# Scores of two chunks made side by side in blocks of 32 keys, from unit two on

## The chip, the cores and the metric

The kernel runs on one core of one Trainium2 chip. The metric is the device time of one execution in microseconds (us); lower is better. TensorE is called PE in the profile (PEld is its weight load), VectorE is DVE, ScalarE is ACT, and SP is the engine whose queue issues the DMAs.

## The reference

Two blocks follow each other. The first is a gated linear recurrence over 768 steps for 4 batches and 8 heads of 48 channels, with a complex decay per channel; the second is a feed-forward block with an unusual activation.

```python
mag = np.sqrt(a_re * a_re + a_im * a_im)
scale = np.minimum(mag, 0.999) / (mag + 1e-06)
a_re_n, a_im_n = (a_re * scale, a_im * scale)
for t in range(S):                       # S = 768, D = 48, B = 4, H = 8
    ar, ai = (a_re_n[:, :, t, :, None], a_im_n[:, :, t, :, None])
    new_re = ar * S_re - ai * S_im
    new_im = ar * S_im + ai * S_re
    kv = np.einsum('bhd,bhe->bhde', k[:, :, t], v[:, :, t])
    S_re, S_im = (new_re + kv, new_im)
    y[:, :, t] = np.einsum('bhd,bhde->bhe', q[:, :, t], S_re)
...
x = np.ascontiguousarray(attn_out.transpose(0, 2, 1, 3)).reshape(B * S, H * D)
h = x @ w_in                             # 3072 x 384 times 384 x 2048
sp = np.maximum(h, 0.0) + np.log1p(np.exp(-np.abs(h)))
g = h * erf(sp)
return (g @ w_out).astype(np.float32)    # 3072 x 2048 times 2048 x 384
```

## The kernel before

The 3072 tokens are worked off in 12 units of 256 tokens; a unit is two chunks of 128 tokens (c = 0 and 1), and three units make one batch. In a chunk the recurrence is a masked product, as in linear attention: queries and keys are multiplied by running products of the decay (`prep`), which makes 96 rows per head (the real and the imaginary part of 48 channels). Their transposes come to stand in the tile `KQ` (96 rows, 16 heads' worth of keys and queries, 128 tokens). From unit 2 on this goes by a 32x32 block transpose on DVE and then 12 DMAs per chunk (`move`, four calls of three DMAs each, one call for each block of 32 tokens).

`scores(u, c, g)` takes one chunk and one group of four heads: four matmuls of 96 rows by 128 keys against 128 queries into one PSUM tile `sc` of the pool `ps_a` (two buffers), and then one DVE product of the whole tile with the upper triangle `triu` (keys not later than the query), written over the keys in `KQ`. A unit has four such steps, named A{u}.{c}.{g}. `state` (S) makes keys times values for a chunk and carries the sum on; `result` (Y) multiplies values with the masked scores, adds state times queries, and writes x transposed. In `state` and `result` the matmuls already have 32 columns in the array, and blocks that belong to different columns follow each other directly.

The feed-forward block of a unit is `ff_in` (h steps, 2 x 3 matmuls with 256 moving columns), activation work on ACT (x, G) and DVE (e), and the output products (O steps; from unit 3 on each is four matmuls of 192 columns, a scheme with seven instead of eight half products). Inputs are 32-bit floats. The profile shows each of these matmuls as two records, so a scores step is 8 records, an O step of units 3 and later 8, an h step 12.

No loop orders the work: the string `ORDER` names some 2,000 step parts, and each name runs the next part of that step's generator. So the order on every engine's queue, SP's included, is the order of that string: the first part of an A step issues the matmuls, the second the DVE product. `v` names load the values of a chunk, `M` names are the calls of `move`, `put` writes 128 tokens of the output with one DMA, and `u` names are matmuls that nobody reads.

Of the kernel before, what the change touches and what calls it, by code (L numbers as in the profile page):

```python
# [54 lines left out]
Q0.1 p0.1 A0.0.1 l1.1 l1.1 kT0.1.0 kT0.1.0 a1.0 l1.1 l1.0 l1.0 a1.1 a1.1 l1.0 A0.0.0 Q0.1 qT0.1.0 qT0.1.0 l1.1 p1.1
p1.1 p1.1 A0.0.0 kT0.1.1 kT0.1.1 a1.1 g2.0 g2.0 qT0.1.1 qT0.1.1 l1.0 p1.0 g2.1 t2 t2 Y0.0 Y0.0 n0 n0 n1 n1 n1 A0.1.0
A0.1.1 g2.1 t2 h0.0.4.0 n1 m2 t2 n5 n5 A0.1.0 n5 s1.0 q1.0 p1.0 Q1.0 n5 p1.0 v0.1 S0.1 k1.0 h0.0.0.0 l2 s1.0 s1.0 Q1.0
qT1.0.0 K1.0 s1.1 r2 A0.1.1 K1.0 n4 n4 p1.0 s1.1 Y0.1 l2 qT1.0.0 p0.1 h0.0.4.0 s1.1 h0.0.0.0 q1.1 Y0.1 Q1.1 qT1.0.1
qT1.0.1 n7 l2 n4 Q1.1 kT1.0.1 kT1.0.1 n4 n7 h0.0.4.1 S0.1 l2 l2 i3 k1.1 i3 kT1.0.0 kT1.0.0 h0.0.0.1 S0.1 h0.0.4.1 K1.1
A1.0.0 n7 v1.0 S1.0 l2 l2 A1.0.1 n6 A1.0.0 n7 n6 p1.1 h0.0.0.1 x0.0 K1.1 n6 A1.0.1 x0.0 x0.0 x0.0 h0.1.0.1 h0.1.0.1  # L60
h0.1.0.0 S1.0 n6 k2.0 p2.0 p2.0 a2.0 a2.0 a2.0 v1.1 S1.1 p1.0 S1.0 p2.0 qT1.1.0 qT1.1.0 kT1.1.1 kT1.1.1 e0.0.0 a2.0
a2.0 a2.0 n11 S1.1 kT1.1.0 e0.0.0 kT1.1.0 a2.0 e0.0.1 n10 v2.1 n10 h0.1.0.0 e0.0.1 G0.0 a2.1 a2.1 a2.1 Y1.0 Y1.0 n10
a2.1 p2.1 p1.1 v3.0 e0.0.0 qT1.1.1 qT1.1.1 h0.1.4.1 h0.1.4.1 A1.1.0 A1.1.0 a2.1 a2.1 a2.1 s2 s2 e0.0.1 A1.1.1 h0.1.4.0
v2.0 A1.1.1 h0.1.4.0 Y1.1 e0.0.1 n10 O0.1 g3.1 e0.0.0 s2 S1.1 Y1.1 g3.0 m3 g3.1 t3 K2.0 h1.0.6 K2.0 K2.0 p2.1 q2.0
# [1405 lines left out]
```

## Time and profile before

| | before |
|---|---|
| median of 3 runs | 641.28 us (640.8 to 641.76) |
| the profiled execution, its own time | 641.29 us |
| its span, first to last instruction | 639.5 us |
| PE busy | 629.0 us (98%), 5464 records |
| DVE busy | 585.5 us (92%) |
| ACT busy | 542.1 us (85%) |

The span is what the trace covers; the 1.8 us between it and the execution's own time lie around it. Busy time of PE includes the modelled ends of pipelined matmuls, so records overlap: what a group of matmuls costs is read from the start of one group to the start of the next, not from a record's duration.

### The profile page before, as it was taken

Reading aid. Unit: us, or ns where it says so; the run is one execution under the profiler, and the core shown is the slowest. Engines: PE = TensorE matmul, PEld = TensorE weight load, DVE = VectorE, ACT = ScalarE, POOL = GpSimd, SP = SyncE. Lnnn points to the kernel's source line nnn. Section 1 sums busy time; section 2 is a strip of 40 time slices with the busy share of each in tenths; the row PEclk is TensorE's granted clock in tenths of the full one; section 3 lists DMA queues with packets and bytes.
Section 4 is the critical chain, followed back from the end, with each engine's and each line's share of the span. In section 5 each row is a group of like instructions: output and inputs, shape, how many; then the busy total and the mean of one; then the engine's idle time right before and its main releaser. Section 6 shows DMA issues by size and latency. Waiting matters only on the chain. (4 is left out here: it accounts for less than half of the span.)

```text
span 639.5 us, 13517 instructions
## 1 busy us (share of the span) xinstructions
PE 629.0 (98%) x5464; PEld 555.0 (87%) x5464; DVE 585.5 (92%) x798; ACT 542.1 (85%) x674; POOL 1.1 (0%) x8
## 2 busy tenths in 40 slices
PE   7799999999999999999999999999999999999998
PEld 7589887877677888999998998898999998999998
DVE  6999999998999999999999799999989999986784
ACT  8999898999999989998894798899799978777840
POOL 0000000000000000000000000000000000000000
PEclk9899999999999999999999999999999999999999
DMA  8887676745357635543526744665564154410023
GB/s 215 196 235 185 143 143 153 209 62 108 57 123 132 179 51 124 107 84 71 99 39 173 149 76 74 155 120 82 127 115 75 26 112 71 73 22 26 1 89 113
DMA packets 282796, 70.27 MB, mean 110 GB/s; under 512 B 269396, under 2 KB 272488, under 8 KB 282728
## 3 DMA queue, kind: packets, MB, share of 16 engines
q1 hardware_dynamic: 282728, 69.36, 50.6%
q8 instruction: 44, 0.72, 0.5%
q14 instruction: 24, 0.20, 0.1%
HBM read 48.82 MB, written 4.75 MB: 84 GB/s over the span
## 5 line engine op out<-in xcount | busy, mean ns | idle before, releaser
L1181 PE MATMUL hps<-xT,w_in_sb 128*128 128x256 f32 (+1 forms) x1248 | 260.8, 364 | 0.3 <-ACT h L1184 0.2
L1181 PEld LDWEIGHTS hps<-xT,w_in_sb 128*128 128x128 f32 x1248 | 220.5, 190 | 29.1 <-ACT h L1184 1.8
L763 ACT ACTIVATE z<-z 128x2048 f32<-128x2048 f32 (+1 forms) x52 | 92.4, 1781 | 9.0 <-DVE e L1212 8.1
L762 ACT ACT_TABLE_LOAD x72 | 92.4, 1283 | 2.1 <-PEq L1454 0.9
L1212 DVE TENSOR_TENSOR e<-z,yy 128x1024 f32<-128x1024 f32 x48 | 58.5, 1218 | 13.1 <-ACT yy L763 12.5
L1184 ACT COPY h<-hps 128x512 f32<-128x512 f32 x96 | 54.3, 580 | 18.5 <-PE hps L1181 18.3
L1252 PE MATMUL ops<-w_out_sb,h 128*128 128x384 f32 x192 | 66.4, 490 | 0.0
L1216 DVE TENSOR_TENSOR z<-z,yy 128x1024 f32<-128x1024 f32 x48 | 58.0, 1219 | 4.4 <-ACT z L763 4.0
L763 ACT ACTIVATE z<-h 128x2048 f32<-128x2048 f32 (+1 forms) x26 | 46.3, 1781 | 15.9 <-DVE h L1218 12.6
L1214 DVE SCALAR_TENSOR_TENSOR yy<-e,yy 128x1024 f32<-128x1024 f32 x48 | 58.7, 1222 | 1.1
L1218 DVE SCALAR_TENSOR_TENSOR h<-z,h 128x1024 f32<-128x1024 f32 x48 | 58.2, 1220 | 1.0
L1252 PEld LDWEIGHTS ops<-w_out_sb,h 128*128 128x128 f32 x192 | 35.5, 190 | 20.9 <-DVE w_out_sb L825 0.6
L1106 PEld LDWEIGHTS sc<-KQ 96*128 96x128 f32 x384 | 48.1, 192 | 5.0 <-ACT KQ L1097 2.4
L1106 PE MATMUL sc<-KQ 96*128 96x128 f32 x384 | 49.8, 276 | 2.2 <-ACT KQ L1097 2.2
L763 ACT ACTIVATE yy<-z 128x2048 f32<-128x2048 f32 (+1 forms) x26 | 46.2, 1778 | 0.6
L763 ACT ACTIVATE yy<-yy 128x2048 f32<-128x2048 f32 (+1 forms) x26 | 46.2, 1777 | 0.5
L1166 PE MATMUL y<-KQ,v 128*32 128x128 f32 x768 | 32.7, 274 | 0.3 <-DVE Skv L1133 0.3
L1110 DVE TENSOR_TENSOR KQ<-sc,triu 128x512 f32<-128x512 f32 x48 | 32.5, 679 | 0.2 <-PE sc L1106 0.2
L1276 PE MATMUL X<-w_out_sb,h 128*128 128x192 f32 x144 | 26.4, 330 | 0.0
L1276 PE MATMUL Y<-T,S 128*128 128x192 f32 x144 | 26.1, 327 | 0.0
L1276 PE MATMUL Z<-T,h 128*128 128x192 f32 x144 | 25.9, 327 | 0.0
L1276 PE MATMUL Y<-w_out_sb,h 128*128 128x192 f32 x144 | 25.7, 326 | 0.0
(125 smaller groups left out, 1011.0 us busy)
## 6 DMA issues: line engine op xcount, KB each, us to landing
KQ<-X SPq DMA_DIRECT2D x240, 64.0 KB, 2.2
raw<-in_moe_w_in_dram SPq DMA_DIRECT2D x8, 768.0 KB
again<-in_moe_w_in_dram SPq DMA_DIRECT2D x8, 768.0 KB, 6.2
raw<-in_moe_w_out_dram SPq DMA_DIRECT2D x8, 768.0 KB, 5.2
ar<-in_a_re_dram SPq DMA_DIRECT2D x24, 192.0 KB, 3.1
ai<-in_a_im_dram SPq DMA_DIRECT2D x24, 192.0 KB, 3.5
v<-in_v_dram SPq DMA_DIRECT2D x48, 96.0 KB, 2.5
k<-in_k_dram SPq DMA_DIRECT2D x24, 192.0 KB, 3.1
```

What stands on the lines that cost most here:

```text
L762: scalar.preload_act_table_set(sets[0])
L763: scalar.activation(func=func, **kw)
L1106: nc.tensor.matmul(out=ps[:, j, :], lhsT=head("k", g * HG + j, u, c), rhs=head("q", g * HG + j, u, c), start=True, stop=True)
L1166: nc.tensor.matmul(out=ps[b * QUAD:(b + 1) * QUAD, i, :], lhsT=lhsT, rhs=rhs, start=start, stop=stop)
L1181: nc.tensor.matmul(out=ps[:, e, :], lhsT=w_in_sb[:, (sl * SLAB + i + e) // 2, kd, e % 2 * P:(e % 2 + 1) * P], rhs=T["xT", u][:, kd, at], s ...
L1184: scalar.copy(out=T["h", u, sl][:, i:i + n, at], in_=ps)
L1212: vector.tensor_tensor(out=t, in0=z, in1=y, op=OP.mult)
L1214: vector.scalar_tensor_tensor(out=y, in0=t, scalar=-2.0, in1=y, op0=OP.add, op1=OP.mult)
L1216: vector.tensor_tensor(out=z, in0=z, in1=y, op=OP.mult)
L1218: vector.scalar_tensor_tensor(out=h, in0=z, scalar=1.0 / RT2, in1=h, op0=OP.add, op1=OP.mult)
L1252: nc.tensor.matmul(out=ps, lhsT=lhsT, rhs=w_out_sb[:, i, :], start=i == HALF, stop=i == KF - 1)
L1276: nc.tensor.matmul(out=ps, lhsT=a(sl)[:, i], rhs=b(sl, i), start=sl == 0 and i == 0, stop=sl == NSL - 1 and i == HALF - 1)
```

## The change

From unit 2 on (`TURNED = 2`) the four steps A{u}.{c}.{g} become two steps A{u}.{g}, each for four heads of both chunks. Each 128x128 product is split into four blocks of 32 keys, which stand in four column groups of the array, and a block is multiplied only with the queries that the mask can keep: 128, 96, 64 and 32 columns. In the second chunk the four blocks of 32 tokens stand in reversed order, so that there the widths are 32, 64, 96 and 128, and each column group has 160 columns for a head of both chunks. Both PSUM buffers of `ps_a` are taken for good (`T["sc"]`), set to zero once, and the parts that no block writes stay zero. The second chunk has a mask of its own, `turned`. `move` writes the second chunk's blocks to reversed places; its values are copied a second time with the rows in reversed blocks (`T["r", u]`, four DMAs from SBUF to SBUF); and its output goes out in four DMAs instead of one. Four smaller buffers hold the values instead of two larger ones. The rounding of the triangle moves into the step `c`. The whole of `ORDER` is replaced by another order; the names in it are else the same.

```diff
 ORDER = """
...
-A8.1.1 A8.1.1 O6.10 O6.11 O6.7 O6.7 O6.11 s9 A8.1.0 g10.1 A8.1.0 Y8 ...
+e7.0.1 e7.0.0 e7.0.0 O6.11 A8.0 A8.0 A8.0 O6.13 e7.0.1 O6.13 A8.1 A8.1 A8.1 Y8 ...
...
-    vbuf = [const.tile([P, C, H // 2, PAIR], FP, name=f"v{i}") for i in range(2)]
+    vbuf = [const.tile([P, H // 2, PAIR], FP, name=f"v{i}") for i in range(2 * C)]
...
+    def blocks(c_turned):
+        n = P // QUAD
+        for i in range(n):
+            j = n - 1 - i if c_turned else i
+            yield slice(i * QUAD, (i + 1) * QUAD), slice(j * QUAD, (j + 1) * QUAD)
+
     def load_v(u, c):
...
         yield
+        if in_turn(u, c):
+            T["r", u] = vbuf[(n + 1) % len(vbuf)]
+            for at, to in blocks(True):
+                nc.sync.dma_start(out=T["r", u][to], in_=t[at])
+            yield
...
     def factors():
-        vector.tensor_scalar(out=turns, in0=triu, scalar1=1.0 / TAU, scalar2=None, op0=OP.mult)
+        vector.tensor_scalar(out=triu_r, in0=turns, scalar1=1.0, scalar2=None, op0=OP.mult)
+        vector.tensor_scalar(out=turns, in0=turns, scalar1=1.0 / TAU, scalar2=None, op0=OP.mult)
         vector.tensor_scalar(out=minus, in0=ident[:, P - 1:P], scalar1=-1.0, scalar2=None, op0=OP.mult)
         yield
-    def rounded_ones():
-        T["triu_r"] = const.tile([P, P], FPR, name="triu_r")
-        vector.tensor_scalar(out=T["triu_r"], in0=triu, scalar1=1.0, scalar2=None, op0=OP.mult)
+        for b in range(P // QUAD):
+            at = slice(b * QUAD, (b + 1) * QUAD)
+            if b > 0:
+                vector.memset(turned[at, 0:b * QUAD], 1.0)
+            vector.tensor_copy(out=turned[at, at], in_=triu[at, at])
+            if b < P // QUAD - 1:
+                vector.memset(turned[at, (b + 1) * QUAD:P], 0.0)
         yield
...
     def move(u, c):
         kq, x = columns(u, c), T["X", (u, c)]
-        for i in range(P // QUAD):
-            at = slice(i * QUAD, (i + 1) * QUAD)
+        for at, to in blocks(in_turn(u, c)):
             for b in range(D2 // QUAD):
-                nc.sync.dma_start(out=kq[b * QUAD:(b + 1) * QUAD, :, at], in_=x[at, b])
+                nc.sync.dma_start(out=kq[b * QUAD:(b + 1) * QUAD, :, to], in_=x[at, b])
             yield
...
+    def scores_side_by_side(u, g):
+        if "sc" not in T:
+            T["sc"] = [ps_a.tile([P, HG, P], FP, tag="a", name="sc") for _ in range(C)]
+            for t in T["sc"]:
+                vector.memset(t, 0.0)
+            yield
+        for j in range(g * HG, (g + 1) * HG):
+            for c in range(C):
+                for b in range(P // QUAD):
+                    at = slice(b * QUAD, (b + 1) * QUAD)
+                    seen_ = slice(0, (b + 1) * QUAD) if in_turn(u, c) else slice(b * QUAD, P)
+                    nc.tensor.matmul(out=T["sc"][c][at, j - g * HG, seen_], lhsT=head("k", j, u, c)[:, at],
+                                     rhs=head("q", j, u, c)[:, seen_], start=True, stop=True)
+        yield
+        for c in range(C):
+            A = T["A", u, c, g] = columns(u, c)[:, g * HG:(g + 1) * HG]
+            mask = turned if in_turn(u, c) else triu
+            vector.tensor_tensor(out=A, in0=T["sc"][c], in1=mask.unsqueeze(1).to_broadcast([P, HG, P]), op=OP.mult)
+            yield
...
-                        both = [(T["v", u][:, c, pair, lo:lo + QUAD], T["A", u, c, g][:, k_, :])]
+                        vs = T["r", u] if in_turn(u, c) else T["v", u, c]
+                        both = [(vs[:, pair, lo:lo + QUAD], T["A", u, c, g][:, k_, :])]
...
     def put(u, jj):
-        nc.sync.dma_start(out=out[t0:t0 + P, :], in_=o[:, jj * DM:(jj + 1) * DM])
+        if not in_turn(u, jj):
+            nc.sync.dma_start(out=out[t0:t0 + P, :], in_=o)
+            return
+        for at, to in blocks(True):
+            nc.sync.dma_start(out=out[t0 + to.start:t0 + to.stop, :], in_=o[at])
```

## Rows read from the trace of the kernel before

**Rows 1.** The page's first part: busy time, share of the span and instructions.
```profile
PE 629.0 (98%) x5464; PEld 555.0 (87%) x5464; DVE 585.5 (92%) x798; ACT 542.1 (85%) x674; POOL 1.1 (0%) x8
```

**Rows 2.** Stretches: us, busy time of each engine, granted clock, DMA share, GB/s.
```profile
200.00:300.00 100.00, 100.00 (x849) 86.38 (x848) 98.26 (x128) 91.53 (x102) 0.00 (x0) 1.00 0.53 110
...
100.00:570.00 470.00, 468.83 (x4003) 410.52 (x4005) 444.13 (x572) 414.65 (x481) 0.00 (x0) 1.00 0.51 101
```

**Rows 3.** Groups by line: busy us, mean ns of one, idle before, what ended it.
```profile
L1106 PE MATMUL sc<-KQ 96*128 96x128 f32 x384 | 49.8, 276 | 2.2 <-ACT KQ L1097 2.2
L1110 DVE TENSOR_TENSOR KQ<-sc,triu 128x512 f32<-128x512 f32 x48 | 32.5, 679 | 0.2 <-PE sc L1106 0.2
```

**Rows 4.** The chain that ended last: start us, its share in us, what.
```profile
527.82 0.60 DVE KQ L1110
...
561.45 0.89 PE sc L1106 x8
562.34 1.30 PE Y L1276 x8
```

**Rows 5.** Timeline of PE, unit 6: start us, us, records merged.
```profile
315.71 1.05 PE L1106 MATMUL sc<-KQ 96*128 96x128 f32 x8
316.60 1.47 PE L1276 MATMUL X<-T,S 128*128 128x192 f32 x8
317.91 1.05 PE L1106 MATMUL sc<-KQ 96*128 96x128 f32 x8
...
318.89 0.84 PE L1127 MATMUL kv<-v,kt 128*32 128x48 f32 x45
319.53 0.30 PE L1166 MATMUL y<-KQ,v 128*32 128x128 f32 x1
319.55 0.22 PE L1127 MATMUL kv<-v,kt 128*32 128x48 f32 x3
319.60 1.27 PE L1166 MATMUL y<-KQ,v 128*32 128x128 f32 x39
320.69 0.62 PE L1166 MATMUL y<-KQ,S 96*32 96x128 f32 x16
321.13 0.62 PE L1166 MATMUL y<-KQ,v 128*32 128x128 f32 x16
...
322.00 0.40 PE L1166 MATMUL y<-KQ,v 128*32 128x128 f32 x8
322.33 1.08 PE L1276 MATMUL W<-w_out_sb,h 128*128 128x192 f32 x5
```

**Rows 6.** Timeline of DVE in the same stretch: the products with the mask.
```profile
319.18 0.67 DVE L1110 TENSOR_TENSOR KQ<-sc,triu 128x512 f32<-128x512 f32 x1
...
320.31 0.67 DVE L1110 TENSOR_TENSOR KQ<-sc,triu 128x512 f32<-128x512 f32 x1
```

**Rows 7.** Timelines of PE and DVE, unit 9, second chunk.
```profile
464.77 1.06 PE L1106 MATMUL sc<-KQ 96*128 96x128 f32 x8
...
471.02 1.95 PE L1106 MATMUL sc<-KQ 96*128 96x128 f32 x16
...
465.87 0.69 DVE L1110 TENSOR_TENSOR KQ<-sc,triu 128x512 f32<-128x512 f32 x1 [0.20 <-PE sc L1106]
...
472.39 1.30 DVE L1110 TENSOR_TENSOR KQ<-sc,triu 128x512 f32<-128x512 f32 x2
```

**Rows 8.** DMA: issues of the moves (median us to landing), SP's timeline, SP's longest wait.
```profile
KQ<-X SPq DMA_DIRECT2D x240, 64.0 KB, 2.2
...
306.44 5.99 SPq L1086 DMA_DIRECT2D KQ<-X  x9
...
SPq L1086 <- DVE X L1075: 67.6, 13, 10.8
```

**Rows 9.** Groups by line on DVE in the first 16 us.
```profile
L915 DVE TENSOR_TENSOR y<-ar 128x384 f32<-128x384 f32 x2 | 1.1, 555 | 2.7 <-DMA ar<-in_a_re_dram 2.7
...
L749 DVE MEMSET v<- 128x128 f32 x2 | 0.3, 165 | 0.0
```

More of the change, by code (lines that the diff above doesn't have):

```diff
@@ L55 @@
[L55 to L64, printed above, removed]
@@ L140 @@
[L140 to L144 removed]
+g0.1 t0.1 t0.1 u8_0 u4_38 g0.0 t0.0 g0.0 H m0.0 c c g0.1 n1 u2_21 m0.1 t0.0 t0.0 t0.1 r0.0 d0.0 u4_2 m0.1 m0.1 n2 r0.1
@@ new lines @@
+e0.0.1 l3 n9 n8 h1.0.6 h1.0.6 a3.0 S1.1 k2.1 K2.1 l3 l3 l3 n9 q2.1 h1.0.0 h1.0.0 a3.0 a3.0 K2.1 O0.1 O0.3 M2.0 M2.0
+M2.0 M2.0 Q2.1 l3 l3 a3.0 n9 Q2.1 h1.0.2 n8 x0.1 x0.1 p3.1 p3.1 p3.1 Q2.1 K2.1 O0.0 n8 a3.1 a3.1 n8 x0.1 x0.1 e0.1.1
+a3.1 q3.0 a3.1 h1.0.4 p3.0 n13 e0.1.1 p3.0 p3.0 M2.1 M2.1 M2.1 e0.1.0 O0.2 n13 A2.0 h1.0.2 O0.4 O0.6 e0.1.0 a3.1
+h1.1.4 M2.1 h1.0.4 O0.5 S2.0 O0.7 p2.0 G0.1 e0.1.0 g4.1 g4.1 a3.1 a3.1 s3 s3 s3 e0.1.0 n13 A2.0 A2.0 A2.0 O0.8 O0.9
+S2.0 e0.1.1 n13 e0.1.1 Q3.0 A2.1 A2.1 Q3.0 k3.0 K3.0 A2.1 g4.0 t4 g4.0 m4 O0.11 x1.0 x1.0 O0.10 t4 n15 n15 v2.1 Y2 Y2
@@ new lines @@
+h4.1.2 e4.0.1 t7 f3.1 g7.1 t7 O2.14 t7 G4.0 O3.0 O3.3 Y5 O3.4 O3.5 K6.0 Y5 v7.0 s6 s6 e4.0.1 e4.0.0 p6.1 O3.7 e4.0.1
+e4.0.1 O3.5 h5.0.0 O3.5 e4.0.0 s6 K6.0 h4.1.2 v6.0 S6.0 O3.5 q6.0 O3.12 O3.13 v6.1 Q6.0 K6.0 Q6.0 r7 i1 i1 l7 l7 O3.4
+k6.1 O3.13 K6.1 i14 x4.1 x4.1 x4.1 h5.0.4 i14 v6.1 K6.1 O3.8 O3.9 O3.10 Q6.0 x4.1 e4.1.1 h5.0.4 h5.0.0 O3.7 O3.7
+e4.1.1 e4.1.0 h5.0.2 l7 l7 l7 G4.1 e4.1.0 e4.1.0 h5.0.2 l7 q6.1 O4.0 h5.0.6 e4.1.1 e4.1.0 e4.1.1 O3.11 O3.11 h5.0.6
+x5.0 x5.0 p6.0 S6.0 x5.0 x5.0 h5.1.0 h5.1.0 f4.0 O4.1 h5.1.4 h5.1.4 Q6.1 f4.1 O4.2 l7 p7.0 p7.1 Q6.1 p7.1 p7.1 M6.0
@@ new lines @@
+x7.0 O6.5 O6.5 O6.5 O6.5 v8.1 p9.1 x7.0 p9.0 p9.0 O6.4 a9.1 a9.1 h7.1.2 h7.1.6 x7.0 q9.0 g10.1 Q9.0 g10.0 t10 t10
+e7.0.1 e7.0.1 a9.1 O6.8 O6.9 O6.10 p9.1 e7.0.0 a9.1 a9.1 M8.1 M8.1 M8.1 M8.1 O6.7 O6.7 G7.0 m10 h7.1.2 e7.0.0 O6.12
+e7.0.1 e7.0.0 e7.0.0 O6.11 A8.0 A8.0 A8.0 O6.13 e7.0.1 O6.13 A8.1 A8.1 A8.1 Y8 s9 s9 s9 O6.11 g10.0 Q9.0 f7.0 O7.1
+g10.1 t10 t10 h7.1.6 x7.1 x7.1 i7 i7 Q9.0 K9.0 Y8 Y8 l10 l10 O7.0 K9.0 K9.0 x7.1 x7.1 e7.1.1 p9.0 O7.1 l10 l10 l10
+v9.0 h8.1.0 h8.1.0 h8.0.6 h8.0.6 e7.1.1 O6.11 e7.1.0 e7.1.0 l10 l10 v9.1 S9.0 G7.1 e7.1.1 e7.1.0 e7.1.0 v9.1 M9.0 M9.0
@@ new lines @@
+M9.0 M9.0 h8.0.4 h8.0.4 h8.0.0 h8.0.0 h8.1.4 e7.1.1 r10 a10.0 a10.0 a10.0 h8.0.2 f7.1 O7.3 a10.0 a10.0 h8.1.4 k9.1
+K9.1 p9.0 S9.0 O7.2 K9.1 a10.0 a10.0 p9.1 q9.1 Q9.1 i8 p9.1 f7.0 p10.1 h8.0.2 k10.0 S9.1 p10.1 i8 O7.2 p10.1 O7.6 Q9.1
+Q9.1 K9.1 x8.0 x8.0 p10.0 O7.4 O7.5 a10.1 a10.1 a10.1 S9.1 S9.1 a10.1 f7.1 h8.1.6 O7.5 q10.0 a10.1 p10.1 x8.0 O6.13
+g11.0 x8.0 p10.0 g11.1 O7.4 O7.7 O7.5 O7.5 O7.7 p10.0 O7.7 t11 e8.0.0 e8.0.0 M9.1 a10.1 e8.0.1 e8.0.1 h8.1.6 K10.0
+a10.1 G8.0 e8.0.0 e8.0.1 h8.1.2 O7.8 O7.9 O7.10 O7.11 h8.1.2 M9.1 M9.1 M9.1 A9.0 A9.0 A9.0 s10 e8.0.0 O7.12 v10.0
@@ new lines @@
+g11.0 s10 s10 e8.0.1 t11 A9.1 k10.1 g11.1 O7.13 x8.1 A9.1 A9.1 Y9 t11 v11.0 Y9 K10.0 S10.0 Q10.0 Q10.0 m11 Y9 h9.0.2
+x8.1 x8.1 O7.13 O7.11 O7.13 f8.0 K10.0 Q10.0 M10.0 M10.0 h9.0.2 f8.0 x8.1 K10.1 t11 l11 M10.0 M10.0 h9.1.4 h9.1.4
+K10.1 h9.0.4 O7.11 e8.1.1 h9.0.4 e8.1.1 e8.1.0 G8.1 l11 h9.0.0 h9.0.0 e8.1.0 O8.1 O8.1 O8.0 e8.1.1 e8.1.1 h9.0.6 k11.0
+r11 e8.1.0 e8.1.0 f8.1 f8.1 l11 l11 K10.1 l11 h9.0.6 x9.0 x9.0 v10.1 q10.1 Q10.1 Q10.1 Q10.1 S10.0 l11 l11 h9.1.0
+h9.1.0 O8.2 O8.6 O8.7 O8.2 O8.3 O8.4 x9.0 x9.0 p10.0 p10.0 S10.0 O8.4 h9.1.6 a11.0 a11.0 e9.0.0 a11.0 a11.0 M10.1
@@ new lines @@
+h10.0.4 h10.0.6 h10.0.6 x10.0 Q11.1 Q11.1 S11.0 h10.1.0 k11.1 K11.1 O9.2 Q11.1 x10.0 x10.0 x10.0 O9.3 O9.4 O9.2 O9.5
+K11.1 K11.1 O9.5 e10.0.1 e10.0.1 h10.1.0 h10.1.2 h10.1.2 p10.1 O8.11 e10.0.0 e10.0.0 O9.5 O9.5 G10.0 M11.1 M11.1
+h10.1.6 M11.1 h10.1.4 h10.1.4 O9.8 O9.9 M11.1 A11.0 e10.0.0 O9.4 e10.0.1 e10.0.1 e10.0.0 h10.1.6 x10.1 x10.1 x10.1
+O9.10 O9.11 O9.6 A11.0 x10.1 S10.1 S10.1 S11.0 f9.1 S11.0 O9.7 A11.0 f10.0 O9.7 A11.1 A11.1 A11.1 O9.7 e10.1.0 e10.1.0
+v11.1 v11.1 Y11 Y11 Y11 e10.1.1 G10.1 O9.12 e10.1.1 h11.0.6 e10.1.1 e10.1.1 e10.1.0 h11.0.6 e10.1.0 h11.0.4 O9.13
@@ new lines @@
+O9.13 f10.1 O9.11 O9.13 h11.0.4 h11.0.2 h11.0.0 x11.0.1 x11.0.1 x11.0.1 x11.0.1 e11.0.1 e11.0.1 h11.0.2 h11.0.0
+x11.0.0 x11.0.0 f10.0 x11.0.0 x11.0.0 f10.1 O9.11 O10.0 O10.3 e11.0.0 G11.0.0 e11.0.0 e11.0.0 h11.1.2 h11.1.2 G11.0.1
+e11.0.1 h11.1.0 h11.1.0 e11.0.0 e11.0.1 O10.1 O10.2 O10.1 h11.1.4 h11.1.6 O10.4 x11.1.0 O10.2 O10.5 O10.4 h11.1.4
+O10.5 O10.5 O10.5 x11.1.0 x11.1.0 h11.1.6 x11.1.0 O10.6 e11.1.0 O10.7 O10.7 O10.7 e11.1.0 x11.1.1 x11.1.1 x11.1.1
+O10.8 O10.9 x11.1.1 e11.1.1 e11.1.1 G11.1.0 e11.1.0 O10.10 O10.11 O10.11 O10.12 O10.11 e11.1.0 G11.1.1 e11.1.1 O10.13
@@ L145 @@
+O10.13 f11.0 O11.0 O11.3 e11.1.1 f11.1 f11.1 O11.1 O11.1 O11.2 O11.2 f11.0 O11.4 O11.4 i10 i10 O10.13 O11.5 O11.5 i12
+O11.6 O11.7 O11.5 O11.5 O11.7 O11.7 i12 Z O11.8 O11.9 O11.10 O11.11 O11.11 Z Z O11.11 O11.12 O11.13 u2_20 u2_40 O11.13
+O11.13
 """
@@ L723, in quotient_path @@
     make_identity(nc, ident)
-    triu = const.tile([P, P], FP, name="triu")
-    make_upper_triangular(nc, triu, val=1.0, diag=True)
+    turns = const.tile([P, P], FP, name="turns")
+    make_upper_triangular(nc, turns, val=1.0, diag=True)
+    triu_r = const.tile([P, P], FPR, name="triu_r")
+    triu = triu_r.bitcast(FP)
+    turned = const.tile([P, P], FP, name="turned")
     column = const.tile([P, 5], FP, name="column")
@@ L729, in quotient_path @@
         vector.memset(t, x)
-    turns = const.tile([P, P], FP, name="turns")
     widths = (NU * C, NU * C, NU * C, NU * NSL + 1, NU * NSL + 1 + C, 18)
@@ L745, in quotient_path @@
     PAIR = 2 * D + GAP
-    vbuf = [const.tile([P, C, H // 2, PAIR], FP, name=f"v{i}") for i in range(2)]
+    vbuf = [const.tile([P, H // 2, PAIR], FP, name=f"v{i}") for i in range(2 * C)]
     sbuf = [const.tile([P, H // 2, PAIR], FP, name=f"S{i}") for i in range(2)]
     for t in vbuf:
-        vector.memset(t[:, :, :, D:D + GAP], 0.0)
+        vector.memset(t[:, :, D:D + GAP], 0.0)
     for t in sbuf:
@@ L784, in load, with in_turn @@
         yield
+    def in_turn(u, c):
+        return u >= TURNED and c == 1
+    def blocks(c_turned):
[3 more added lines that the diff above has]
+            yield slice(i * QUAD, (i + 1) * QUAD), slice(j * QUAD, (j + 1) * QUAD)
     def load_v(u, c):
-        t = T["v", u] = vbuf[u % 2]
+        n = C * u + c if u < TURNED else C * TURNED + (C + 1) * (u - TURNED) + c
+        t = T["v", u, c] = vbuf[n % len(vbuf)]
         for e in range(2):
             src = rows(v, u, c).rearrange("t (h e) d -> e t h d", e=2)[e]
-            nc.sync.dma_start(out=side(t[:, c], e), in_=src)
+            nc.sync.dma_start(out=side(t, e), in_=src)
         yield
+        if in_turn(u, c):
[3 more added lines that the diff above has]
+            yield
     N = 2 * DM
@@ L875, in quotient_path @@
     ALL = (0, C)
+    TURNED = 2
     TURNS, HALVED, LATE = 2, 2, 0
@@ L889, in factors @@
     def factors():
-        vector.tensor_scalar(out=turns, in0=triu, scalar1=1.0 / TAU, scalar2=None, op0=OP.mult)
+        vector.tensor_scalar(out=triu_r, in0=turns, scalar1=1.0, scalar2=None, op0=OP.mult)
+        vector.tensor_scalar(out=turns, in0=turns, scalar1=1.0 / TAU, scalar2=None, op0=OP.mult)
         vector.tensor_scalar(out=minus, in0=ident[:, P - 1:P], scalar1=-1.0, scalar2=None, op0=OP.mult)
         yield
-    def rounded_ones():
-        T["triu_r"] = const.tile([P, P], FPR, name="triu_r")
-        vector.tensor_scalar(out=T["triu_r"], in0=triu, scalar1=1.0, scalar2=None, op0=OP.mult)
+        for b in range(P // QUAD):
[5 more added lines that the diff above has]
+                vector.memset(turned[at, (b + 1) * QUAD:P], 0.0)
         yield
     def running(ps, hi, lo):
-        nc.tensor.matmul(out=ps, lhsT=T["triu_r"], rhs=hi, start=True, stop=False)
-        nc.tensor.matmul(out=ps, lhsT=T["triu_r"], rhs=lo, start=False, stop=True)
+        nc.tensor.matmul(out=ps, lhsT=triu_r, rhs=hi, start=True, stop=False)
+        nc.tensor.matmul(out=ps, lhsT=triu_r, rhs=lo, start=False, stop=True)
     def g_mag(u, cc=ALL):
@@ L1127, in state @@
                 nc.tensor.matmul(out=kv[b:b + QUAD, j, :], lhsT=keys[:, b:b + QUAD],
-                                 rhs=side(T["v", u][:, c, j // 2], j % 2), start=True, stop=True)
+                                 rhs=side(T["v", u, c][:, j // 2], j % 2), start=True, stop=True)
         yield
@@ L1378, in quotient_path @@
                 steps["S" + at] = state(u, c)
-            for g in range(NHG):
+            for g in range(NHG if u < TURNED else 0):
                 steps[f"A{at}.{g}"] = scores(u, c, g)
             steps["a" + at], steps["p" + at] = g_angle(u, c), g_decay(u, c)
+        for g in range(NHG if u >= TURNED else 0):
+            steps[f"A{u}.{g}"] = scores_side_by_side(u, g)
         for at, cc in [(f"{u}.{c}", (c, c + 1)) for c in range(C)] if u < 2 else [(f"{u}", ALL)]:
@@ L1405, in quotient_path @@
             steps[f"O{u}.{i}"] = f
-    steps["Z"], steps["j"], steps["c"] = check(), rounded_ones(), factors()
+    steps["Z"], steps["c"] = check(), factors()
     with tc.manual_schedule():
```

142 lines of the change are left out of this document (56 added, 86 removed).

## The prediction, made blind

> **What bounds the kernel now.** I read the busy shares first, then the table of stretches, then the chain that ended last, then the timelines of PE and DVE around a unit's scores. PE is busy 98% of the span, DVE 92% [rows 1]. The mean hides two stages, so look at the middle: from 100 to 570 us PE is busy 468.8 of 470 us at the full granted clock, DVE 444.1 (25.9 us free), ACT 414.7 [rows 2]. There a microsecond less of PE work can be a microsecond less of time, but only while DVE keeps up, and between 200 and 300 us DVE is 98.3% busy itself [rows 2]. The chain's end is PE's work, scores steps at 0.89 us each in it [rows 4]. So the question has two halves: what PE saves, and whether the tighter coupling between PE and DVE gives it back.
>
> **What goes.** 40 of the 48 scores steps (10 units, four each) at 0.89 us: 35.6 us of PE. The 384 records of the group are 8 to a step, 0.111 us apart, though each record lasts 0.276 us [rows 3, 4].
>
> **What comes.** 20 steps of four heads for both chunks, 64 records each, with 32, 64, 96 or 128 moving columns in four column groups. The trace has no such mix, but it has its ends. With 128 columns and 32-column weights, 16 records of `y` go from 320.69 to 321.13: four turns of four side by side, 0.110 us a turn [rows 5]. With 48 columns, 48 records of `kv` go from 318.89 to the `y` at 319.60: 16 turns of three, 0.044 us a turn [rows 5]. A straight line through these gives 0.084 for 96, 0.057 for 64 and 0.031 for 32 columns. A column group has per head 128+32 or 96+64, both 0.141 us, twice (two records per matmul): 0.282. 20 x 4 x 0.282 = 22.6 us. Bounds: if 32 columns cost no less than 48 do, 110+44 makes 0.308 per head and 24.6 us; in proportion to columns alone, 0.275 and 22.0 us. I take the line, since both its ends are measured.
>
> Does a group go on with its next block while another is busy? In program order every `kv` matmul stands ahead of `y`; yet one `y` record starts at 319.53, before the last three of `kv` at 319.55 [rows 5]. `kv` uses three column groups, and the fourth was free. So the groups don't wait for each other, and unequal widths can balance over the two chunks, which is what the reversed order asks for.
>
> The Trainium skill (TensorE: Matmul & The Clock Gate, section "The mechanism") says otherwise: matmuls start and end strictly in program order, whatever tile they are in. By the row above this doesn't hold here for starts; by the rule, each chunk's four blocks would end with the widest, and the scores would cost as much as before.
>
> **Switching.** Going from a full-width step into 32-column ones costs: `sc` at 317.91 would be through 0.89 us later, at 318.80, and `kv` starts at 318.89, 0.09 us. Out again: the 8 records of `y` at 322.00 take two turns, to 322.22, and W starts at 322.33, 0.11 us [rows 4, 5]. 0.20 us for each run of 32-column steps. Reading the steps that use PE out of both order strings: S and Y stand in 31 such runs before, S, Y and A in 40 after (many new A steps adjoin a Y or S). 9 x 0.20 = 1.8 us.
>
> PE's sum: -35.6 + 22.6 + 1.8 = -11.2 us (with the bounds -11.8 to -9.2).
>
> **The new wait.** Before, a scores step takes one of two PSUM buffers, so PE needs DVE's product of two steps ago. After, a step takes both buffers, and the next step waits for both products of this one; everything behind it on PE's queue waits too. How late is DVE? Call lag the time from the end of a step's records (start plus 0.89) to the start of its product. In unit 6: 316.60 to 319.18, 2.6 us, and 318.80 to 320.31, 1.5 us [rows 5, 6]. In unit 9: 465.66 to 465.87, 0.2 us, where DVE stood waiting for it; 471.91 to 472.39, 0.5 us; and the second of that pair 0.2 [rows 7]. Before the change a lag costs nothing.
>
> Where does it cost after? In the new order, units 6 to 10 have a single O step (1.30 us [rows 4]) between A{u}.0 and A{u}.1, so PE is back after 1.30 + 0.20 = 1.50 us; the products take 0.60 each [rows 4]; with a hand-off of 0.2 back to PE (taken from the one the other way [rows 7]) the stall is lag + 1.2 + 0.2 - 1.5 = lag - 0.1. In units 4, 5, 7, 8 and 11 Y stands directly behind A{u}.1. Y takes the first heads first and needs heads 4 to 7 after three of its turns of four matmuls, 24 records or six turns of 0.110 = 0.66 us; the stall is lag + 0.6 + 0.2 - 0.66 = lag + 0.14. Ten places: ten times the lag, + 0.2 us. With the hand-off alone (0.2) that is 2.2 us; with 1.5 it is 15.2 us. I take 0.4, nearer to the low end, because a PE that waits lets DVE catch up, so late DVE can't be paid in full at each place. 4.2 us.
>
> **Parts costed at nothing.** The mask, rounding and `turned` work is some ten more small DVE instructions at the start, under 0.165 us each (the 128x128 memset), while DVE waits 2.7 us for the first gates [rows 9]; without that cover under 1.7 us. Clearing the two score tiles is eight times that memset's area at most, under 1.4 us, once, out of DVE's 25.9 us. The products with the mask are as many and as large as before. SP gets 40 copies of values and 30 more output DMAs. A move costs SP 0.67 us of issue (9 in 5.99 [rows 8]), so up to 4.7 us per unit. They hide as long as SP waits for others: its moves alone waited 67.6 us for DVE's transposes [rows 8]. What is late if they don't: in unit 6 the last move is issued at 312.43 and lands 2.2 us later at 314.6; the second chunk's scores start at 315.71 [rows 5, 8]. 1.1 us of slack. In the new order several of the copies (v9.1, say) stand directly ahead of moves, and there a copy also waits on SP for its load to land.
>
> **The number.** The profiled execution took 641.29 us (span 639.5 and 1.8 around it), which is the median of the runs. 641.3 - 11.2 + 4.2 = 634.3 us. The start and the end of the span, where PE waits, I leave as they are: the same work stands there in another order, and no row says which way that goes.
>
> **The rivals.**
>
> *DVE sets the pace (other side).* The ten waits cost what the lags of unit 6 say: at 1.5 us 15.2, thus 645.3 us. It decides from a lag of 1.1 us on, where 10 x 1.1 + 0.2 = 11.2 eats the gain. For it: DVE's 98.3% in the second hundred us, and lags of 1.5 and 2.6. Against: DVE has 5.5% free over the middle, and a wait of PE shortens the next lag. Chance 0.22.
>
> *No stall worth counting.* With the hand-off alone and some of it covered, 0 to 2.2 us: 630.1 to 632.3, and 629.5 with the low bound of the matmuls. For it: the lags of unit 9. Chance 0.12.
>
> *The split brings nothing.* Blocks of a chunk end together: 2 x 2 x 0.110 = 0.440 us per head, 35.2 us for all, -35.6 + 35.2 + 1.8 = +1.4, and with the stalls 646.9 us. If only starts are in order, the next chunk's first block is held back, 0.33 per head and 26.4 us: 638.1. The `y` record ahead of `kv` [rows 5] speaks against both. Chance 0.06. The rule of the Trainium skill (TensorE: Matmul & The Clock Gate, "The mechanism") would make it so.
>
> *SP is late.* 4.7 us more issue per unit against 1.1 us of slack: up to 3.6 us of late scores in each of 10 units, 36 us; if it strikes one unit in five, 7.2 us, thus 641.5. For it: the copies ahead of moves; against: SP's long waits for DVE, which show that it is ahead. Chance 0.10.
>
> **Chances and range.** The forecast, 631 to 638 us, has 0.50. I call faster what is below 640.0 and slower what is above 642.6, 0.2% either way, about what a measurement of this kernel can tell from no change. Faster: 0.50 + 0.12 + 0.02 (starts in order) + 0.02 (SP, rarely) = 0.66. Same: 0.07 of late DVE and 0.05 of SP = 0.12. Slower: 0.15 + 0.04 + 0.03 = 0.22. Cases of both signs hold weight, so the range reaches from the low bound without much stall, 629, to late DVE, 646; the likeliest case's own range is 631 to 638.
>
> **What would show it.** A scores step of the new kind from start to the next PE step in some 1.2 to 1.4 us; 1280 records of it; PE idle ahead of A{u}.1 and Y ended by the DVE product, a few us in all; DVE's share of the middle risen to some 96%. Wrong would be: a step of 1.8 us (no overlap), PE idle of over 11 us behind the products, or idle ended by the DMA into `KQ` or by the copied values.

## The result, and the profile after

| | before | after |
|---|---|---|
| median (4 runs each, same chip) | 641.11 us (640.8 to 641.76) | 631.33 us (629.56 to 632.67) |
| ratio, 95% interval | | 0.9844 (0.9819 to 0.987) |
| the profiled execution, its own time | 641.29 us | 631.1 us |
| its span | 639.5 us | 629.3 us |

The change saves 9.8 us. The forecast was 634.3 us, so 3.0 us more came than was foreseen; the time lies just inside the likeliest case's own range.

The first part of the page after, to be read against [rows 1]:

```profile
PE 618.6 (98%) x6424; PEld 543.6 (86%) x6424; DVE 584.9 (93%) x812; ACT 541.8 (86%) x674; POOL 1.1 (0%) x8
```

PE lost 10.4 us of busy time and the span 10.2, although PE has 960 records more: the scores are now many short records. DVE has as much to do as before and its share rose. The stretches that answer to [rows 2]:

```profile
200.00:300.00 100.00, 100.00 (x1064) 86.64 (x1064) 98.65 (x131) 95.13 (x109) 0.00 (x0) 1.00 0.54 109
100.00:570.00 470.00, 468.56 (x5104) 407.64 (x5103) 450.52 (x580) 421.28 (x486) 0.00 (x0) 1.00 0.54 108
```

PE is the bound as before, at the full granted clock, and DVE is closer to it: 450.5 of 470 us (96%), where it had 444.1. So DVE has some 19 us free in the middle.

The groups of the new scores and their products (compare [rows 3]):

```profile
L1143 PE MATMUL sc<-KQ 96*32 96x64 f32 (+3 forms) x1280 | 27.0, 235 | 0.0
L1149 DVE TENSOR_TENSOR KQ<-sc,turned 128x512 f32<-128x512 f32 x20 | 13.6, 679 | 0.0
```

A product with the second mask takes 679 ns, as one with the first did. What a step costs is read from PE's timeline. Here are the two steps of unit 5, with the first record behind Y of that unit, and the two of unit 6 (start us, us, engine, line, operation, records merged):

```profile
249.81 1.33 PE L1143 MATMUL sc<-KQ 96*32 96x128 f32 x64
251.07 2.87 PE L1320 MATMUL Y<-T,S 128*128 128x192 f32 x16
253.87 1.33 PE L1143 MATMUL sc<-KQ 96*32 96x128 f32 x64
255.00 0.42 PE L1206 MATMUL y<-KQ,v 128*32 128x128 f32 x8
...
258.93 1.24 PE L1320 MATMUL Y<-w_out_sb,h 128*128 128x192 f32 x6
...
307.89 1.33 PE L1143 MATMUL sc<-KQ 96*32 96x128 f32 x64
309.16 1.57 PE L1320 MATMUL Y<-w_out_sb,h 128*128 128x192 f32 x8
310.65 1.33 PE L1143 MATMUL sc<-KQ 96*32 96x128 f32 x64
311.92 1.57 PE L1320 MATMUL X<-T,S 128*128 128x192 f32 x8
```

From 253.87 to the `y` at 255.00 a step takes 1.13 us (1.138 by the unrounded starts). The forecast was 1.128. Where a full-width O step follows, it is 1.26 us (249.81 to 251.07). DVE's timeline beside the two steps of unit 5:

```profile
251.70 0.68 DVE L1149 TENSOR_TENSOR KQ<-sc,triu_r 128x512 f32<-128x512 f32 x1
252.30 0.68 DVE L1271 TENSOR_TENSOR h<-h 128x512 f32<-128x512 f32 x1
252.90 0.68 DVE L1149 TENSOR_TENSOR KQ<-sc,turned 128x512 f32<-128x512 f32 x1
...
255.21 0.69 DVE L1149 TENSOR_TENSOR KQ<-sc,triu_r 128x512 f32<-128x512 f32 x1 [0.43 <-PE sc L1143]
255.81 0.68 DVE L1149 TENSOR_TENSOR KQ<-sc,turned 128x512 f32<-128x512 f32 x1
```

The first step's product starts 0.6 us after the next PE step began, the second's 0.2 us, and there it is DVE that stood waiting for PE. The waits of the whole span (us in total, times, longest):

```profile
PEld sc L1143 <- issue: 4.5, 14, 0.5
DVE KQ L1149 <- PE sc L1143: 2.3, 6, 0.7
...
PEld sc L1143 <- DVE KQ L1149: 1.4, 5, 0.5
...
PEld y L1206 <- DVE KQ L1149: 0.9, 5, 0.2
```

"issue" is time in which the engine waited for nothing that the profile shows. The weight loads (PEld) stood idle for the products 1.4 us before a scores step and 0.9 us before `y`. PEld works ahead of PE, so this is not yet time that PE lost. Ahead of a scores step it is none: in units 6 to 10 PEld is idle for 0.2 us before the second step whether a product or "issue" is named, and the full-width step in between takes 1.50 us up to the second scores step each time (309.16 to 310.65 in unit 6). In Y, which needs the products of the later heads only after its first matmuls, some time is lost: in unit 5 Y takes 3.92 us from its first record to the next step (255.00 to 258.93), and 3.65 us in experiment 1 below, where no such wait is listed. Added up over the five units in which Y stands directly behind the scores, this is some 1.2 us more than in experiment 1. No wait of PE for the DMAs into `KQ` or for the copied values is listed.

One more wait is new. Behind the first two of the new steps, in unit 2, the output products wait for DVE:

```profile
110.18 1.33 PE L1143 MATMUL sc<-KQ 96*32 96x128 f32 x64
111.79 2.85 PE L1296 MATMUL ops<-w_out_sb,h 128*128 128x384 f32 x8 [0.27 <-DVE h L1258]
114.56 1.33 PE L1143 MATMUL sc<-KQ 96*32 96x128 f32 x64
116.33 1.88 PE L1296 MATMUL ops<-w_out_sb,h 128*128 128x384 f32 x5 [0.43 <-DVE w_out_sb L840]
```

From step to step these two take 1.61 and 1.77 us where the others take 1.26: 0.8 us more. The issues of DMAs that came new:

```profile
v<-v SPq DMA_DIRECT2D x40, 56.0 KB
out_dram<-out SPq DMA_DIRECT2D x40, 48.0 KB
```

### The profile page after: what moved, and what is told of

The parts are those of the page before. It is cut to its first block, busy times and chain, and to the rows that moved or that the text cites. A ratio compares the mean times of both kernels' runs of the same rounds, so it can differ in the third digit from the quotient of the medians.

```text
span 629.3 us, 15561 instructions
## 1 busy us (share of the span) xinstructions
PE 618.6 (98%) x6424; PEld 543.6 (86%) x6424; DVE 584.9 (93%) x812; ACT 541.8 (86%) x674; POOL 1.1 (0%) x8
## 4 chain that ended last, share of the span: by engine, by line
PE 77%; DVE 13%; DMA 4%; SPq 3%; issue 3%; ACT 0%; DVEq 0%
PE hps L1221 30%; PE ops L1296 8%; PE Z L1320 8%; PE Y L1320 7%; PE X L1320 7%; PE y L1206 6%; PE W L1320 4%; PE sc L1143 4%; PE kv L1166 2%; DVE word L838 2%; SPq L1105 1%; DMA again<-in_moe_w_out_dram 1%; DMA raw<-in_moe_w_out_dram 1%; DVE word L835 1%; DVE w_in_sb L840 1%
## 5 line engine op out<-in xcount | busy, mean ns | idle before, releaser
L1206 PE MATMUL y<-KQ,v 128*32 128x128 f32 x768 | 35.8, 274 | 0.1
L1143 PEld LDWEIGHTS sc<-KQ 96*32 96x32 f32 x1280 | 23.9, 110 | 6.6 <-issue 4.5
L1206 PE MATMUL y<-KQ,S 96*32 96x128 f32 x640 | 27.8, 272 | 0.0
L1206 PEld LDWEIGHTS y<-KQ,v 128*32 128x32 f32 x768 | 24.6, 110 | 3.6 <-issue 1.8
L1143 PE MATMUL sc<-KQ 96*32 96x64 f32 (+3 forms) x1280 | 27.0, 235 | 0.0
L1320 PE MATMUL W<-w_out_sb,h 128*128 128x192 f32 x144 | 26.4, 332 | 0.0
```

What stands on the lines that cost most here:

```text
L1143: nc.tensor.matmul(out=T["sc"][c][at, j - g * HG, seen_], lhsT=head("k", j, u, c)[:, at], rhs=head("q", j, u, c)[:, seen_], start=True, st ...
L1206: nc.tensor.matmul(out=ps[b * QUAD:(b + 1) * QUAD, i, :], lhsT=lhsT, rhs=rhs, start=start, stop=stop)
L1320: nc.tensor.matmul(out=ps, lhsT=a(sl)[:, i], rhs=b(sl, i), start=sl == 0 and i == 0, stop=sl == NSL - 1 and i == HALF - 1)
```

## The experiments

The first four ran on one chip beside a median before of 641.33 us, the next four beside 641.01, the last two beside 640.75.

**1. The new order without the blocks.** Both chunks in one step, both buffers, reversed tokens, copies and order as in the change, but one full 128x128 product per head and chunk.

```diff
-                for b in range(P // QUAD):
-                    at = slice(b * QUAD, (b + 1) * QUAD)
-                    seen_ = slice(0, (b + 1) * QUAD) if in_turn(u, c) else slice(b * QUAD, P)
-                    nc.tensor.matmul(out=T["sc"][c][at, j - g * HG, seen_], ...)
+                nc.tensor.matmul(out=T["sc"][c][:, j - g * HG, :], lhsT=head("k", j, u, c),
+                                 rhs=head("q", j, u, c), start=True, stop=True)
```

> The changed kernel in all but one thing: each head's scores are one matmul of 128 keys by 128 queries again (the new order, both PSUM buffers per step and the reversed blocks of the second chunk stay). Theory (the blocks save PE time and the time follows PE): a step goes from 1.13 to 16 records x 0.111 = 1.78 us, 20 x 0.65 = 13 us more, less some 2 us of switching into and out of 32-column steps, so about 11 us more than the changed kernel, near 642 us. Rival (the new order made the gain, not the blocks): about 631 us, as the changed kernel.

Measured: 637.62 us, ratio 0.9951 (0.9934 to 0.9967). The page of this kernel:

```profile
PE 625.6 (98%) x5464; PEld 556.8 (88%) x5464; DVE 585.1 (92%) x812; ACT 542.3 (85%) x674; POOL 1.1 (0%) x8
```

So 3.7 us of the gain come without any block, with the same number of PE records as before, and the blocks themselves are worth 637.62 - 631.33 = 6.3 us. Neither expectation had both parts. Y of unit 5 in this kernel:

```profile
257.38 0.43 PE L1203 MATMUL y<-KQ,v 128*32 128x128 f32 x8
...
261.03 1.24 PE L1317 MATMUL Y<-w_out_sb,h 128*128 128x192 f32 x6
```

**2. No reversal.** The blocks of both chunks in natural order, no second copy of the values (its ten names are left out of `ORDER` too), one output DMA per chunk: column group 0 then has 128 + 128 columns per head, group 3 has 32 + 32.

```diff
     def in_turn(u, c):
-        return u >= TURNED and c == 1
+        return False
```

> The blocks stay, but the second chunk keeps its natural order: widths 128, 96, 64, 32 in both chunks, no copied values, one output DMA per chunk. Theory (a column group runs through its own blocks, and the fullest group sets a step's length): the first group has 2 x 128 columns per head, 4 x 4 x 0.110 = 1.76 us per step in place of 1.13, so 12.6 us more than the changed kernel, near 644 us, no better than before. Rival (the number of matmuls or their mean width sets the price, 80 columns as in the changed kernel): a step of 1.13 us and 631 us, or a little less for the DMAs saved.

Measured: 640.04 us, ratio 0.9984 (0.9974 to 0.9993). PE's timeline in unit 5:

```profile
253.39 1.94 PE L1143 MATMUL sc<-KQ 96*32 96x128 f32 x64
255.26 2.87 PE L1320 MATMUL Y<-T,S 128*128 128x192 f32 x16
258.06 1.83 PE L1143 MATMUL sc<-KQ 96*32 96x128 f32 x63
259.61 0.31 PE L1206 MATMUL y<-KQ,v 128*32 128x128 f32 x3
259.72 0.27 PE L1143 MATMUL sc<-KQ 96*32 96x128 f32 x1
```

The step that took 1.26 us to the next O step takes 1.87 (253.39 to 255.26). Twenty steps are some 12 us more, of which 8.7 show in the time. The fullest column group sets the length. Without the reversal the blocks bring nothing: against experiment 1, the same order without blocks, they cost 2.4 us (640.04 against 637.62). The second step also shows the groups apart: three records of `y` start ahead of the last one of `sc`, which stands before them in the program.

**3. Chunk after chunk.** The same blocks and widths, but all four heads of the first chunk before those of the second.

```diff
-        for j in range(g * HG, (g + 1) * HG):
-            for c in range(C):
+        for c in range(C):
+            for j in range(g * HG, (g + 1) * HG):
```

> The same blocks with the same widths, only issued in another order: all four heads of the first chunk, then all four of the second, where the changed kernel goes from chunk to chunk head by head. A step's total per column group is the same. Theory (a group runs ahead of the others only by the few matmuls that PE holds ready): the first chunk is paced by its widest blocks, 4 x 2 x 0.110 = 0.88 us, the second too, 1.76 us in all less what is held ready, say 1.5 to 1.7; 631 + 20 x 0.4 to 0.6 = 639 to 643 us. Rival (groups run wholly on their own): 1.13 us per step and 631 us.

Measured: 636.79 us, ratio 0.9935 (0.9916 to 0.9955). PE's timeline in unit 5:

```profile
250.19 1.76 PE L1143 MATMUL sc<-KQ 96*32 96x128 f32 x64
251.88 2.87 PE L1320 MATMUL Y<-T,S 128*128 128x192 f32 x16
```

1.69 us to the O step, between the 1.26 of the changed kernel and the 1.87 of no balance. A free column group does run ahead of a busy one, but only by some matmuls: the second chunk's wide blocks can't start early enough to fill the groups that the first chunk leaves empty. The alternation of chunks within each head is worth 5.5 us. That is less than the 8 to 12 us of the expectation: where `y` follows, as behind the second step of unit 5, it starts 1.17 us after the step's start, ahead of the step's last records, so there little is lost.

**4. Without the additional DMAs.** The 40 copies of values and the 30 more output DMAs are left out.

```diff
-            T["r", u] = vbuf[(n + 1) % len(vbuf)]
-            for at, to in blocks(True):
-                nc.sync.dma_start(out=T["r", u][to], in_=t[at])
...
-        if not in_turn(u, jj):
+        if True:
             nc.sync.dma_start(out=out[t0:t0 + P, :], in_=o)
```

> The 40 copies of values into reversed rows and the 30 additional output DMAs are left out: the second chunk multiplies its values in their natural row order and its output leaves in one DMA, so those outputs aren't the reference's. Theory (the 70 DMAs are hidden, SP has room): 631 us within 1.5. Rival (SP's 4.7 us of issue per unit delays the moves and through them the scores): 3 to 10 us faster than the changed kernel, 621 to 628 us.

Measured: 630.78 us, ratio 0.984 (0.9824 to 0.9857), against 0.9844 (0.9819 to 0.987) with them. They are hidden.

**5. The changed kernel again,** beside the next kernels.

> The changed kernel itself, unchanged, beside the others on the same chip: 631.3 us within 1.5.

Measured: 631.16 us, ratio 0.9837 (0.9824 to 0.985).

**6. Late products.** The two products of A{u}.0 in units 6 to 10 stand behind the other DVE work of that stretch, directly ahead of A{u}.1.

```diff
-h6.1.6 A7.0 A7.0 A7.0 O6.0 s8 Q8.0 Q8.0 A7.1 A7.1 A7.1 h6.1.6 x6.1
+h6.1.6 A7.0 O6.0 s8 Q8.0 Q8.0 A7.0 A7.0 A7.1 A7.1 A7.1 h6.1.6 x6.1
```

> In units 6 to 10 the two products of a unit's first scores step are moved on DVE behind the other DVE work that stands between the two scores steps, directly ahead of the second. No work is added. Some 9 us of DVE work in five places goes ahead of products for which PE waits. Theory (PE waits for both products): PE idle ahead of these five steps grows by 5 to 9 us, and the time by most of it, 635 to 640 us. Rival (the wait is hidden or given back at once, since DVE's other work is then done earlier): 631 to 632 us.

Measured: 640.73 us, ratio 0.999 (0.998 to 0.9999). Its waits:

```profile
PEld sc L1142 <- DVE KQ L1148: 9.9, 12, 2.1
...
PE sc L1142 <- DVE KQ L1148: 6.4, 10, 1.8
```

The wait of the forecast is a real one: with five pairs of products further back in DVE's queue 9.6 us are lost (640.73 against 631.16), a little more than the expected range. The two rows overlap in time and can't be added: PE itself waits 6.4 us for the products, 0.4 us in experiment 5. What the rest of the 9.6 us is, is not split up here. The changed kernel is spared because its order puts the products early.

**7. Four fewer runs of 32-column steps.** S6.1 next to S7.0, and the O steps that stood between A{u}.1 and Y in units 6, 9 and 10 ahead of A{u}.1; 40 runs become 36.

```diff
-a7.0 a7.1 A6.1 A6.1 O4.4 A6.1 p7.0 a7.1 O4.5 O4.5 O4.5 O4.5 O4.7 k7.0 Y6
+a7.0 a7.1 O4.5 A6.1 A6.1 O4.4 A6.1 p7.0 a7.1 O4.5 O4.5 O4.5 O4.7 k7.0 Y6
```

> The changed kernel with four names moved in the order, so that 32-column steps adjoin: S6.1 goes next to S7.0, and in units 6, 9 and 10 the O step between A{u}.1 and Y goes ahead of A{u}.1. 40 runs of 32-column steps become 36, at 0.2 to 0.3 us a run 0.8 to 1.2 us less. Theory (switching costs that, and two O steps cover the products of A{u}.0 better, while Y has less cover): 0 to 1.5 us faster than the changed kernel, 630 to 631.5. Rival (Y waits longer than is saved): 631.5 to 634.

Measured: 635.97 us, ratio 0.9916 (0.9902 to 0.993), 4.8 us slower than experiment 5. That is slower than both expectations. Its waits:

```profile
DVE KQ L1148 <- PE sc L1142: 4.6, 7, 2.4
...
PEld y L1205 <- DVE KQ L1148: 2.3, 8, 0.6
...
PE kv L1165 <- DVE kt L1088: 1.1, 1, 1.1
```

The O step that filled the time in which DVE makes the product now stands ahead of the scores. So DVE waits longer for the scores (4.6 us against 2.3), and the weight loads of `y` longer for the products (2.3 against 0.9). Once PE also waits 1.1 us ahead of the matmuls of `state` for DVE's `kt`, a wait of PE that experiment 5 doesn't list. Moving four names so as to save four runs loses more than it brings. How much of the 4.8 us each of the four names costs is not settled.

**8. The steps of the change in the order of before.** Each new step stands where the second chunk's old step stood.

```diff
-q7.0 A6.1.1 p7.1 g8.0 O4.5 O4.5 a7.1 a7.1 A6.1.0 A6.1.0 S6.1 S6.1 h5.1.2 h5.1.6 A6.1.1 x5.1
+q7.0 A6.1 p7.1 g8.0 O4.5 O4.5 a7.1 a7.1 A6.0 A6.0 A6.0 S6.1 S6.1 h5.1.2 h5.1.6 A6.1 A6.1 x5.1
```

> The changed kernel with the order of before: a unit's new scores steps stand where the steps of its second chunk stood, those of the first chunk are dropped, the copies of values are put in behind the moves, and six loads of values stand later, so that four buffers do. PE's work is that of the changed kernel within 0.5 us (39 runs of 32-column steps for 40). Theory (the wait for both products is what the order has to cover): in units 2, 5, 7, 9 and 10 the two steps of a unit stand directly behind each other here, so PE waits lag + 1.2 + 0.2 us each, at a lag of 0.2 to 2 us 8 to 17 us in all: 638 to 648 us. Rival (the order is of no matter, the blocks make the gain): 631 to 634 us.

Measured: 683.65 us, ratio 1.0662 (1.0647 to 1.0678). The direction was as expected (638 to 648 us), the size much larger. In this order some products stand behind the matmuls of the next step, which the next kernel mends.

**9. The same with each step's products ahead of the next step's matmuls.**

```diff
-A6.1 p7.1 g8.0 O4.5 O4.5 a7.1 a7.1 A6.0 A6.0 A6.0 S6.1 S6.1 h5.1.2 h5.1.6 A6.1 A6.1 x5.1
+A6.1 p7.1 g8.0 O4.5 O4.5 a7.1 a7.1 A6.1 A6.1 A6.0 A6.0 A6.0 S6.1 S6.1 h5.1.2 h5.1.6 x5.1
```

> The old order with the new steps once more, as in the run before it, but with the products of a scores step always ahead of the next step's matmuls in the order (in that run some stood behind, so that the second step overwrote what the first one's product still had to read, and its scores were not the reference's). Theory (the old order does not cover the wait for both products and for the first chunk's later scores): PE idle behind the products of tens of us, 665 to 690 us. Rival (the misplaced products or the broken scores alone made that run slow): 631 to 650 us.

Measured: 699.67 us, ratio 1.0932 (1.091 to 1.0953). That is above the expected range, and slower than experiment 8, so the misplaced products are not what made that run slow. Its waits:

```profile
PEld sc L1142 <- DVE KQ L1148: 28.3, 18, 6.2
PE sc L1142 <- DVE KQ L1148: 22.8, 12, 6.1
```

Three stretches of it (us, busy time of PE, PEld, DVE, ACT, POOL, granted clock, DMA share, GB/s):

```profile
260.00:280.00 20.00, 14.63 (x120) 11.32 (x119) 17.45 (x22) 18.91 (x25) 0.00 (x0) 1.00 0.50 111
280.00:300.00 20.00, 18.70 (x249) 16.86 (x250) 16.62 (x23) 11.33 (x13) 0.00 (x0) 0.83 0.37 72
300.00:320.00 20.00, 20.00 (x153) 18.69 (x152) 15.68 (x23) 16.92 (x18) 0.00 (x0) 1.00 0.35 74
```

PE's timeline in unit 5, and the stretch of its second step:

```profile
273.92 1.33 PE L1142 MATMUL sc<-KQ 96*32 96x128 f32 x64
281.30 2.85 PE L1142 MATMUL sc<-KQ 96*32 96x128 f32 x64 [6.05 <-DVE KQ L1148]
284.08 1.33 PE L1319 MATMUL Y<-T,S 128*128 128x192 f32 x3
...
281.30:284.10 2.80, 2.80 (x65) 2.02 (x65) 2.77 (x6) 2.62 (x3) 0.00 (x0) 0.50 1.02 204
```

The second step waits 6.05 us for the products of the first, and then takes 2.78 us where the changed kernel takes 1.26: after PE had idled, the granted clock of the step's own stretch is 0.50, the lower level of 1.2 GHz, and the mean over the 20 us around it 0.83. Over the whole run the mean granted clock is 0.968, in the changed kernel 0.997. So a wait costs its own length and then the slow work behind it.

**10. Experiment 9 with full 128x128 products** (the edit of experiment 1).

> The kernel of the run beside it (old order, two chunks per step), with each head's scores as one matmul of 128 by 128 again. PE has some 10 us more work. Theory (what the blocks save is worth its full size only where PE sets the pace): 0 to 6 us slower than the run beside it, since PE waits for DVE there anyway. Rival (the saving is additive in any order): 8 to 12 us slower.

Measured: 708.16 us, ratio 1.1036 (1.1005 to 1.1067). The blocks save 8.5 us here, as much as in the good order or more: the rival was right. So the short steps are not what loses time in the old order, which is as slow without them. The longest wait of PE that is listed is the one for the products in the shared pair of buffers (22.8 us in experiment 9, 19.9 here). How the rest of the loss divides among the lower clock, the other waits and the later scores of the first chunk is not settled.

## Why the prediction was right, and where it was off

**The new step was right.** 22.6 us were predicted for 20 steps; 20 x 1.138 = 22.8 us were measured. Its two assumptions were tried apart. That the column groups don't wait for each other: the step of experiment 2 takes what its fullest group needs (1.87 us to the O step, 16 records of 0.110 and 0.13 for the way out being 1.89), the balanced one 1.26. That the reversal makes the balance: 8.7 us by experiment 2. The rival that the split brings nothing falls with it. The Trainium skill (TensorE: Matmul & The Clock Gate, "The mechanism") has matmuls start and end strictly in program order; the trace of experiment 2, with `y` at 259.61 ahead of `sc` at 259.72, doesn't agree. The Trainium skill (TensorEngine Tiling (Array Packing), "Key Properties") also calls the tiles independent of each other; the same rows agree with that, up to the limit that experiment 3 shows.

**The lag was over-sized.** The term "ten times the lag, + 0.2 us", 4.2 us with a lag of 0.4, cost PE some 1.2 us, all of it in Y: less than the hand-off alone was to cost (2.2 us). That is the condition of the rival *No stall worth counting*, which had a chance of 0.12, and the time lies in its range too (630.1 to 632.3). The lags of unit 6 in the old order, 1.5 and 2.6 us, belonged to products for which nothing waited. In the new order the products stand early, and at six steps DVE stood waiting for the scores (2.3 us). The rival that DVE sets the pace is a true mechanism, shown by experiment 6 (640.7 us) and experiment 9 (699.7); this order keeps out of its reach.

**Switching was under-sized.** 0.20 us per run was taken, 0.09 in and 0.11 out. Read from unit 5 after: out of the step 1.264 - 1.138 = 0.13 us more than into `y`. Then the 16 records of Y to the next step, 251.07 to 253.87, take 2.80 us where two O steps take 2.60 [rows 4]: 0.20, for the way into the next step and a delay behind the way out. That is 0.33 us a run, and 9 x 0.33 = 3.0 us in place of 1.8. The delay could have been read before: in the W of unit 6 that follows `y` at 322.33, the second record starts 0.27 us after the first, and the later ones 0.16 us apart. The prediction read only up to the first.

**The new order itself was left out of the sum.** With the measured sizes, and the 0.8 us of waits behind the first two steps, for which the prediction had no term, the sum is -35.6 + 22.8 + 3.0 + 1.2 + 0.8 = -7.8 us, and -9.8 was measured. Experiment 1 holds what is missing: in it PE's steps cost as before and the time is 3.7 us shorter. Counted in the two orders, S, Y and A stand in 26 runs of 32-column steps when A is full-width, where before they stood in 31; five runs are 1.6 us, which the 3.0 us already contain. The other 2.1 us are the order's, and what they consist of is not settled. -7.8 - 2.1 = -9.9. The prediction put the new order's own worth at nothing ("no row says which way that goes"); with this 2.1 us and the lag 4.2 - 1.2 = 3.0 us the forecast was too high, and with the switching 1.2, the step 0.2 and the waits in unit 2 0.8 us too low. These errors cancel in part: that the time lies inside the likeliest case's own range, 0.3 us above its end, is partly luck.

By the same numbers the blocks alone, from experiment 1 to the change, go from 26 runs to 40: 20 steps of 16 records at 0.111 us are 35.5 us, so -35.5 + 22.8 + 14 x 0.33 + 1.2 + 0.8 = -6.1; 6.3 was measured.

**SP was hidden,** as costed: experiment 4 differs by 0.55 us from the changed kernel, within the intervals, and no wait of PE for a moved block or copied value is listed.

No version tried here is faster than the changed kernel by more than the intervals.

## What to carry to other kernels

Cutting a triangular product into blocks of 32 columns in the array paid here only with the same number of moving columns for each column group, and in full only with blocks that alternate so that a group's next block stands near in the program. Where two steps came to share buffers, the price of the change was set by where the consumer of the first stands in its queue: keep it early there, and keep other work for the producer between the two steps. A wait that the profile lists for the weight loads is not yet a loss: look whether PE's own records come later for it. Before moving a name that looks free, ask which engine was working behind it.

## What the hardware showed that was not expected

- Leaving 32-column work costs twice: 0.13 us at once, and about 0.10 us more inside the full-width group that follows (0.20 us in all over the 16 records of Y, the way in at its end included). The kernel before shows the same delay behind `y`: 0.27 us from the first to the second record of W, 0.16 us between later ones.
- A column group runs ahead of the others only by a little: chunk after chunk, 1.69 us to the next O step, where unlimited freedom would have given 1.26 and none, by an estimate of 2 x 0.88 + 0.13, 1.89.
- Where PE had waited 6.05 us, a scores step ran at a granted clock of 0.50 and took 2.78 us instead of 1.26; the mean over the 20 us around it was 0.83. In the changed kernel the middle shows 1.00 throughout.
